# Retention and MLP kernel: one cast moved to VectorE, batch 1's steps and two turns shifted in the weave

## The chip, the cores and the metric

The kernel runs on one core of a Trainium2 chip. Its time is the device time of one execution in microseconds. TensorE (PE in the profile) does the matrix products and the transposes, VectorE (DVE), ScalarE (ACT) and GpSimd (POOL) do elementwise work, and SP issues most of the DMAs; ScalarE issues some too. Each engine works through its own list of instructions in order and waits in front of an instruction until the semaphores that it needs have been raised. So an instruction that waits also holds up everything behind it on its engine.

## The reference

Two layers follow each other. The first is a retention (a linear attention with a decaying state) over 4 batches, 8 heads, 768 positions and 64 channels per head. The second is a mixer: a low-rank mixing over the positions, then an MLP.

```python
for t in range(S):
    state = gamma * state + einsum('bhd,bhe->bhde', k[:, :, t], v[:, :, t])
    y[:, :, t] = scale * einsum('bhd,bhde->bhe', q[:, :, t], state)

# x: y with the heads side by side, [batch, 768, 512]; rank 32, d_model 512
h  = (x.T @ U @ V).T            # mixing over the 768 positions
u  = x + h
out = u + relu(u @ w_ch1) @ w_ch2      # 512 -> 2048 -> 512
```

## The kernel before, in words

The 768 positions of a batch are taken in chunks of 128. Within a chunk, scores of q and k are masked (the masked scores are called `a`) and multiplied by v, and a running state, which is copied from PSUM to SBUF after each chunk, carries what came before. The decay is folded into q and k by the tables `gq` and `gk`.

**The order is written by hand.** The schedule is manual: the order in which the Python code calls the engines is the order in each engine's list.

*Start, batch 0.* Nothing else can run yet, so batch 0 is taken in three blocks of 256 positions (`sc` = 0, 1, 2; lines 784 to 816). Per block, `prep_pair` and `prep_block` (line 240) scale k and q and cast v from fp32 to bf16 in two halves of four heads; the letters passed say which engine takes which half (P GpSimd, D VectorE, A ScalarE). `turn_block` transposes k and q on TensorE. `state_half` (line 346) adds half a block to the state in one PSUM bank and copies it to SBUF on ScalarE; the next `state_half` adds to the same bank and needs that copy to be done, and it needs both halves of the cast v. `score_block` makes the scores and masks them; `mix_block` (line 392) makes the outputs x. Then come the low-rank step and the first up products.

*The weave, batches 0 to 3.* For b = 1 to 4 the loop at line 850 calls `weave` (line 743). It takes the MLP of batch b-1 as a list of pieces with a cost in microseconds (an up product of 128 of the 2048 channels over 512 positions costs 0.864, over the last 256 positions 0.432, a part of a down product 0.864 or 0.874) and puts the steps of other tracks between them: a step with mark d runs before the first piece at which the summed cost has reached d times the total. The total is 41.47 for batch 0's MLP (16 x 0.864 + 16 x 0.432 + 24 x 0.864) and about 39.1 for the others. The tracks are:
- `first`: the low-rank step for u's last two chunks of batch b-1 (`lr_expand`, positions 512 to 767; VectorE adds it to x, line 517), and their turn into `uT`, which the up products over the last 256 positions read. For b = 1 and 2 TensorE turns (`lr_turn_pe`, line 529, with a copy on ScalarE), for b = 3 and 4 a transposing DMA on SP does (`lr_turn`, line 544).
- batch b's own retention, chunk by chunk: `prep_chunk` (line 258, GpSimd), the turn of q and k (`turn_pe` at line 424 for b = 1; a transposing DMA, `turn_dma` at line 432, on ScalarE's queue for b = 2 and on SP's for b = 3), `state`, `score`, `mix`, at the marks `at[i]` plus 0, `lag[0]`, `lag[1]`, `lag[2]`. Below, (b,i) is chunk i of batch b.
- for b = 1, `order_v` (a reordering copy on GpSimd) and eight subtractions on VectorE (`w2_sums`, line 552) that prepare the weights of a seven-product scheme for the later down products.
- the low-rank step of batch b (`lr_open`, `lr_proj`, `lr_expand`, `lr_turn_pair` for b = 1), at marks that follow from the last `at`.

The stores of finished output rows wait in a list. `weave` issues those that were in the list when a piece began right after that piece, so their place between the other DMAs of SP's queue depends on the marks as well: batch 0's rows go out in two stores of 128 KB per chunk on SP.

*Loads.* All inputs pass through a ring of 16 SBUF tiles. `feed_one` (line 123) puts the next load into SP's list each time a tile has been used up, in a fixed order: the blocks of batch 0, U and V, w1, the first chunk of batch 1, w2, then q, k, v of every further chunk.

*Banks.* PSUM has eight banks. The up products of batches 1 to 3 (`up`, line 671) turn over four of them (`RINGS["mlp"]`); three of four results are taken out by a relu on ScalarE (line 684), every fourth by VectorE (line 682). Where such a relu comes late, TensorE finds no free bank.

Of the kernel before, what the change touches and what calls it, by code (L numbers as in the profile page):

```python
# [18 lines left out]
def kernel(  # L19
# [11 lines left out]
    nc = tc.nc  # L31
    P = 128
    B, H, S, D = q.shape
# [18 lines left out]
    SEVEN = 1  # L52
# [70 lines left out]
    def feed_one():  # L123
        if n_fed[0] == len(feed):
            return
        key, src = feed[n_fed[0]]
        n_fed[0] += 1
        if key[0] == "uv":
            nc.sync.dma_start(
                out=Uf.rearrange("p s two r -> p s (two r)"),  # L130
                in_=moe_U.rearrange("(s p two) r -> p s (two r)", p=P, two=2))
            nc.sync.dma_start(
                out=Vf, in_=moe_V.rearrange("r (f t) -> (r f) t", f=NSC))
            return
        t = rin.tile([P, 512], fp32, tag="in", name=f"in_{n_fed[0]}")
        ready[key] = t
        if key[0] in "qkv":
            t = t.rearrange("p (h d) -> p h d", h=H if len(key) == 3 else 4)
        nc.sync.dma_start(out=t, in_=src)

    def take(*key):
        assert feed[n_used[0]][0] == key, (feed[n_used[0]][0], key)
        n_used[0] += 1
        return ready.pop(key, None)
# [24 lines left out]
    def keep_busy(n, fresh=False):  # L169
        if fresh:  # L170
            idle_bank[0] = bank("mlp")
        for i in range(4 * n):
            nc.tensor.matmul(idle_bank[0][:, ts(i % 4, P)], ones[:, :P],  # L173
                             ones[:, :P], start=True, stop=True,
                             skip_group_check=True)
# [53 lines left out]
    for i in range(NST):  # L229
        t = consts.tile([P, 4, P], bf16, name=f"state{i}")  # L230
# [9 lines left out]
    def prep_block(eng, nm, sc, hh):  # L240
        if hh == 0:
            pre[nm, sc] = blk.tile([P, 2, H, D], bf16, tag=nm + "0",
                                name=f"{nm}0_{sc}")
        t = pre[nm, sc][:, :, ds(4 * hh, 4)]
        src = take(nm, 0, sc, hh).rearrange("p (h two d) -> p two h d", h=4,
                                            two=2)
        if nm == "v":
            if eng == "A":
                nc.scalar.activation(t, src, AF.Copy)
            else:  # L250
                nc.gpsimd.tensor_copy(out=t, in_=src)
        else:
            g = (gq0 if nm == "q" else gk0)[:, sc, :, ds(4 * hh, 4), None]
            (nc.gpsimd if eng == "P" else nc.vector).tensor_tensor(
                t, src, g.to_broadcast([P, 2, 4, D]), op=ALU.mult)
        feed_one()
# [16 lines left out]
    def prep_uv():  # L273
        take("uv")
        nc.gpsimd.tensor_copy(out=Uh, in_=Uf)
        nc.gpsimd.tensor_copy(
            out=Vh.rearrange("p (x two t) -> p x two t", x=2, two=2),
            in_=Vf.rearrange("p (x t two) -> p x two t", x=2, two=2))
        feed_one()
# [48 lines left out]
    def turn_block(nm, sc, eng):  # L328
        src = pre[nm, sc]
        t = blk.tile([P, 4, 2, P], bf16, tag=nm + "T0",  # L330
                      name=f"{nm}T0_{sc}")
        np_ = 4 // len(eng)
        for g in range(len(eng)):
            tp = bank("mlp", bf16)
            for p in range(np_):
                for par in range(2):
                    nc.tensor.transpose(
                        tp[:, ds(2 * P * p, 2 * P)].rearrange(
                            "p (x two m) -> p two x m", x=2, two=2)[:, par],
                        src[:, par, ds(2 * (np_ * g + p), 2)], ident)  # L340
            evac(eng[g], t[:, ds(np_ * g, np_)],
                 tp[:, :2 * P * np_].rearrange("p (n x m) -> p n x m", n=np_,
                                               x=2))
        live[nm, sc] = t
# [206 lines left out]
    def part(f, *args):  # L551
        return lambda: f(*args)
# [221 lines left out]
    def prep_pair(nm, sc, engs):  # L774
        for hh in range(2):
            prep_block(engs[hh], nm, sc, hh)
# [7 lines left out]
    for sc in range(NSC):  # L784
        last = sc + 1 == NSC
        keep_busy(3 if sc else 9, fresh=not last)
        turn_block("k", sc, "D")
        keep_busy(0 if sc else 7)
        turn_block("q", sc, "AD" if last else "A")
        prep_pair("v", sc, "PA")  # L790
        if sc:
            state_half(sc - 1, 1)
        else:
            keep_busy(4)
        score_block(sc, 0)
        if last:
            prep_uv()
        else:
            prep_pair("k", sc + 1, "PD")
            prep_block("P", "q", sc + 1, 0)  # L800
            keep_busy(0 if sc else 3)
        if sc:
            score_block(sc, 1, "mlp", "DA")
        else:
            score_block(sc, 1)
        if last:
            state_half(sc, 0)
            mix_block(sc - 1, "AD")
            continue
        prep_block("D", "q", sc + 1, 1)  # L810
        if sc:
            mix_block(sc - 1, "AA")
        keep_busy(4 if sc else 1, fresh=sc > 0)
        state_half(sc, 0)
        if sc == 0:
            nc.vector.tensor_scalar(mask, jmat, srange, None, op0=ALU.is_ge)
# [23 lines left out]
    for c in range(NCB):  # L840
        evac("AD"[c % 2], uTs[0][:, :NLO, c], four(xT[c]))
    keep_busy(3)
    first = [part(lr_expand, 0, 4, 2), part(lr_turn_pe, 0, 4),
             part(lr_expand, 0, 0, 4)]
# [5 lines left out]
    for b in range(1, B + 1):  # L850
        tracks = []
        if b > 1:
            old = b - 1 < SEVEN
            first = [part(lr_expand, b - 1, 4, 2, "qk" if old else "st"),
                     part(lr_turn_pe, b - 1, 4, "qk" if old else "o")
                     if b < 3 else part(lr_turn, b - 1, 4)]
            if not old:
                RINGS["mlp"] = [6, 0, 1, 2]
        tracks.append((first, 0.02, 0.2 if b - 1 < SEVEN else 0.06))
        if b < B:  # L860
            if b == 1:
                at = [0.455, 0.555, 0.61, 0.67, 0.725, 0.78]
                lag = [0.01, 0.035, 0.065]
                turn = turn_pe
                for i in range(AHEAD, NCK):
                    tracks.append(([part(prep_chunk, b, i)], at[i] - 0.1, 1))
                tracks.append(([order_v], at[-1] - 0.05, 1))
                for f, d in zip(w2_sums(0) + w2_sums(2),
                                (0.495, 0.51, 0.53, 0.58, 0.635, 0.65, 0.695,
                                 0.71)):  # L870
                    tracks.append(([f], d, d))
            else:
                for i in range(NCK):
                    prep_chunk(b, i)
                at = [0.04 + 0.085 * i for i in range(NCK)]
                lag = [0.12, 0.17, 0.23] if b == 2 else [0.1, 0.12, 0.2]
                if b == 2:
                    for i, f in enumerate(w2_sums(4) + w2_sums(6)):
                        d = 0.04 + 0.025 * i
                        tracks.append(([f], d, d))  # L880
                turn = turn_dma
            for i in range(NCK):
                for f, d in ((turn, 0), (state, lag[0]), (score, lag[1]),
                             (mix, lag[2])):
                    tracks.append(([part(f, b, i)], at[i] + d, at[i] + d))
            t = at[-1] + lag[2]
            if b == 1:
                tracks += [([part(lr_open, b), part(lr_proj, b)], t + 0.02,
                            t + 0.02),
                           ([part(lr_expand, b, 0, 4)], t + 0.04, t + 0.04),  # L890
                           ([part(lr_turn_pair, b, 0, "A"),
                             part(lr_turn_pair, b, 2, "D")], t + 0.08, t + 0.12)]
            else:
                for fs, d in (([part(lr_open, b), part(lr_proj, b)], 0.03),
                              ([part(lr_grow, b, 0, 4, "st")], 0.06),
                              ([part(lr_add, b, 0, 4, (0, 1))], 0.06),
                              ([part(lr_add, b, 0, 4, (2, 3))], 0.11),
                              ([part(lr_turn, b, 0)], 0.17),
                              ([part(lr_turn, b, 2)], 0.171)):
                    tracks.append((fs, t + d, t + d))  # L900
        weave(mlp_pieces(b - 1), *tracks)
# [29 lines left out]
```

## Time and profile before

| what | us |
|---|---|
| median of 5 runs | 226.78 (225.72 to 226.98) |
| the profiled execution | 226.79 |
| its span, first to last instruction | 225.0 |
| TensorE busy | 213.7 |
| VectorE busy | 147.0 |
| ScalarE busy | 89.1 |
| GpSimd busy | 84.4 |

The page gives the busy time of each engine, a strip of 40 slices of the span, the DMA queues, the chain of work that ended last and the costliest groups of instructions. The trace behind it can be asked for the waits (who waited for whom), for the instructions of a stretch in order of time, and for one line. In those rows "L677" is a line of the kernel, `gT<-mlp` says what is written and read, and `[0.50 <-ACT state L85]` says how long the engine stood before and what is taken to have released it. Releasers are inferred. Further lines that come up: 357 and 444 are the state's matmuls in batch 0 and later, 460 the scores, 465 their masks, 480 the products of masked scores with v in `mix`, 538 the turn of u's first four chunks, 727 VectorE's sum for a finished chunk of batch 0's output, 781 the making of a selection table on VectorE. Helpers share lines: line 85 is every copy out of PSUM on ScalarE, line 87 every one on VectorE.

Time is measured from the span's start: the first up product of the MLP starts at 28.26 us, the first down piece of batch 0 at 51.47, the up products of batch 1 at 82.89, those of batch 2 at 134.8 and those of batch 3 near 181.7.

### The profile page before, as it was taken

To read this page: it belongs to the slowest core of one execution; us is meant where nothing else is said; L and a number is where in the kernel's file an instruction comes from. 1 tells how busy PE (TensorE), PEld (TensorE's weight loads), DVE (VectorE), ACT (ScalarE), POOL (GpSimd) and SP (SyncE) were. 2 spreads that over 40 slices of the span, in tenths; PEclk is the share of its full clock that TensorE was granted. 3 is DMA by queue.
4 is the path that set the end of the run, shared out by engine and by line. 5 is a ranking of instruction groups with operands and counts; after the bars stand their busy time and mean duration, and the time that the engine had idled before them with its cause. 6 is when DMAs were issued, how large, how long until landed. Compare 5 with 4: busy or idle time off the path is not lost. (4 is left out here: it accounts for less than half of the span.)

```text
span 225.0 us, 5592 instructions
## 1 busy us (share of the span) xinstructions
PE 213.7 (95%) x2275; PEld 150.1 (67%) x2275; DVE 147.0 (65%) x292; ACT 89.1 (40%) x183; POOL 84.4 (38%) x123
## 2 busy tenths in 40 slices
PE   6899999999999999699999999999999999999993
PEld 6777844595565454366678884766888855668882
DVE  7678556326873569599997744697777542867452
ACT  3257554464555125376721004776410035551000
POOL 6447878788687856324648202000000000000000
PEclk9999999999999999999999999999999999999999
DMA  6998999999999999999999389921001822000023
GB/s 181 299 291 240 293 368 221 373 338 197 222 208 191 219 207 232 258 192 191 236 208 217 137 177 222 193 44 35 3 0 53 213 112 47 0 1 3 37 106 139
DMA packets 93370, 38.84 MB, mean 173 GB/s; under 512 B 76864, under 2 KB 86176, under 8 KB 93344
## 3 DMA queue, kind: packets, MB, share of 16 engines
q1 hardware_dynamic: 86144, 35.33, 65.4%
q10 hardware_dynamic: 7200, 3.15, 6.7%
q8 instruction: 18, 0.29, 0.6%
q14 instruction: 8, 0.07, 0.1%
HBM read 27.46 MB, written 6.29 MB: 150 GB/s over the span
## 5 line engine op out<-in xcount | busy, mean ns | idle before, releaser
L677 PE MATMUL mlp<-uT,w1b 128*128 128x512 f16 (+1 forms) x512 | 89.7, 326 | 2.4 <-ACT gT L684 2.2
L684 ACT ACTIVATE gT<-mlp 128x512 f16<-128x512 f32 (+1 forms) x94 | 45.6, 490 | 65.9 <-PE mlp L677 60.8
L677 PEld LDWEIGHTS <-w1b 128*128 128x128 f16 x512 | 47.9, 98 | 32.9 <-issue 2.4
L682 DVE TENSOR_SCALAR gT<-mlp 128x512 f16<-128x512 f32 (+1 forms) x34 | 18.9, 555 | 28.0 <-PE mlp L677 28.0
L599 PEld LDWEIGHTS <-gT 128*128 128x128 f16 x288 | 27.6, 98 | 3.6
L268 POOL TENSOR_TENSOR qkd<-in,gk 128x512 bf16<-128x512 f32 x18 | 19.8, 1099 | 22.6 <-DMA in<-in_k_dram 22.4
L465 DVE TENSOR_TENSOR a<-s,mask 128x512 bf16<-128x512 f32 x36 | 23.1, 683 | 6.6 <-PE s L460 6.6
L722 PE MATMUL mlp<-w2b,gT 128*128 128x512 f16 x96 | 23.9, 380 | 0.0
L268 POOL TENSOR_TENSOR qkd<-in,gq 128x512 bf16<-128x512 f32 x18 | 19.4, 1079 | 11.3 <-DMA in<-in_q_dram 8.5
L599 PEld LDWEIGHTS <-gS 128*128 128x128 f16 x216 | 21.0, 98 | 3.2 <-issue 0.5
L85 ACT ACTIVATE x<-o 128x512 f16<-128x512 f32 x20 | 11.9, 595 | 20.6 <-PE o L480 20.2
L599 PE MATMUL A<-w2t,gT 128*128 128x256 f16 x144 | 18.4, 273 | 0.0
L85 ACT ACTIVATE state<-st 64x256 bf16<-64x256 f32 x40 | 15.0, 374 | 4.4 <-PE st L357 3.1
L722 PEld LDWEIGHTS <-gT 128*128 128x128 f16 x96 | 8.1, 98 | 7.7
L266 POOL CAST vd<-in 128x512 bf16<-128x512 f32 x18 | 11.2, 624 | 4.5 <-DMA in<-in_v_dram 3.1
L173 PE MATMUL mlp<-ones 128*128 128x128 bf16 x136 | 10.3, 238 | 1.4 <-DVE ones L166 1.4
L173 PEld LDWEIGHTS <-ones 128*128 128x128 bf16 x152 | 9.9, 107 | 2.2 <-DVE ones L166 1.4
L320 POOL CAST w2b<-in 128x512 f16<-128x512 f32 x16 | 9.8, 614 | 2.9 <-DMA in<-in_moe_w_ch_dram 2.2
L517 DVE TENSOR_TENSOR x<-s,x 128x256 f16<-128x256 f32 (+1 forms) x16 | 8.2, 552 | 4.2 <-PE st L511 1.9
L314 POOL CAST w1b<-in 128x512 f16<-128x512 f32 x16 | 9.6, 613 | 2.8 <-DMA in<-in_moe_w_ch_dram 2.3
L85 ACT ACTIVATE qkT<-qk 128x1024 bf16<-128x1024 bf16 x6 | 6.1, 1023 | 8.2 <-PE qk L424 8.1
L599 PE MATMUL B<-w2b,gT 128*128 128x256 f16 x72 | 9.3, 273 | 0.0
(135 smaller groups left out, 274.8 us busy)
## 6 DMA issues: line engine op xcount, KB each, us to landing
in<-in_moe_w_ch_dram SPq DMA_DIRECT2D x32, 256.0 KB, 6.2
in<-in_k_dram SPq DMA_DIRECT2D x24, 256.0 KB, 5.5
in<-in_q_dram SPq DMA_DIRECT2D x24, 256.0 KB, 5.5
in<-in_v_dram SPq DMA_DIRECT2D x24, 256.0 KB, 5.4
out_dram<-o SPq DMA_DIRECT2D x12, 256.0 KB, 2.0
out_dram<-o SPq DMA_DIRECT2D x12, 128.0 KB, 3.5
out_dram<-o ACTq DMA_DIRECT2D x6, 256.0 KB, 2.6
Uf<-in_moe_U_dram SPq DMA_DIRECT2D x1, 96.0 KB, 4.6
```

The source lines that it names most:

```text
L85: nc.scalar.activation(dst, src, AF.Copy)
L173: nc.tensor.matmul(idle_bank[0][:, ts(i % 4, P)], ones[:, :P], ones[:, :P], start=True, stop=True, skip_group_check=True)
L266: nc.gpsimd.tensor_copy(out=t, in_=src)
L268: nc.gpsimd.tensor_tensor(t, src, g[:, ci, :, None].to_broadcast([P, H, D]), op=ALU.mult)
L314: nc.gpsimd.tensor_copy(out=w1b[:, c, ts(mb, 512)], in_=take("w1", mb, c))
L320: nc.gpsimd.tensor_copy(out=w2b[:, m], in_=take("w2", m))
L465: nc.vector.tensor_tensor(a, four(sp[i]), causal(mask), op=ALU.mult)
L599: nc.tensor.matmul(acc[key, i], lhs[:, m, ts(i, P)], rhs[:, m], start=(fresh and m == 0), stop=(m == NH - 1), skip_group_check=True)
L677: nc.tensor.matmul(g_p[:, :sz], w1b[:, c, ts(m, P)], uTs[b][:, ds(j, nj), c], start=(c == 0), stop=(c == NCB - 1))
L682: nc.vector.tensor_relu(gT[:, m, ds(lo, sz)], g_p[:, :sz])
L684: nc.scalar.activation(gT[:, m, ds(lo, sz)], g_p[:, :sz], AF.Relu)
L722: nc.tensor.matmul(ch, gT[:, m, ts(j, P)], w2b[:, m], start=(m == 0), stop=(m == NM - 1))
```

## The change

Four edits, none of which alters what is computed:
- In the last block of batch 0 (`sc` = 2) the second half of the v cast moves from ScalarE to VectorE. ScalarE's list then has the copy of the state right after its share of the q turn; VectorE's list has the cast after its own share of the q turn and ahead of the masks.
- For b = 1 the marks of the six chunks move from 0.455, 0.555, ... to 0.475, 0.575, ..., that is by 0.02 of the weave. The preparation of chunks 1 to 5, `order_v` and the low-rank step of batch 1 are tied to these marks and move with them.
- For b = 1 the eight subtractions of `w2_sums` move by 0.02 as well.
- The track `first` ends at 0.14 for b = 2 and at 0.1 for b = 3 instead of 0.06. Its second step, the turn of u's last two chunks, comes halfway through the track, so its mark moves from 0.04 to 0.08 (b = 2, from two pieces in to four) and from 0.04 to 0.06 (b = 3, from two pieces in to three). For b = 1 and b = 4 nothing changes there.

```diff
             if eng == "A":
                 nc.scalar.activation(t, src, AF.Copy)
             else:
-                nc.gpsimd.tensor_copy(out=t, in_=src)
+                (nc.vector if eng == "D" else nc.gpsimd).tensor_copy(out=t,
+                                                                     in_=src)
...
         turn_block("q", sc, "AD" if last else "A")
-        prep_pair("v", sc, "PA")
+        prep_pair("v", sc, "PD" if last else "PA")
         if sc:
             state_half(sc - 1, 1)
...
-        tracks.append((first, 0.02, 0.2 if b - 1 < SEVEN else 0.06))
+        tracks.append((first, 0.02, (0.2, 0.14, 0.1, 0.06)[b - 1]))
         if b < B:
             if b == 1:
-                at = [0.455, 0.555, 0.61, 0.67, 0.725, 0.78]
+                at = [0.475, 0.575, 0.63, 0.69, 0.745, 0.8]
                 lag = [0.01, 0.035, 0.065]
...
                 for f, d in zip(w2_sums(0) + w2_sums(2),
-                                (0.495, 0.51, 0.53, 0.58, 0.635, 0.65, 0.695,
-                                 0.71)):
+                                (0.515, 0.53, 0.55, 0.6, 0.655, 0.67, 0.715,
+                                 0.73)):
                     tracks.append(([f], d, d))
```

## The prediction

> **What bounds the kernel now.** First the engines of the page, then the table of waits, then the timeline at the waits that are not matmuls.
>
> ```profile
> PE 213.7 (95%) x2275; PEld 150.1 (67%) x2275; DVE 147.0 (65%) x292; ACT 89.1 (40%) x183; POOL 84.4 (38%) x123
> ```
>
> TensorE works for 213.7 of 225.0 us at full clock. The change takes no matmul away, so only the 11.3 us in which TensorE stands can shrink. Of the rows of the waits with PE in front, these lie near the edits (waiter and releaser, total us, times, longest):
>
> ```profile
> PE mlp L677 <- ACT gT L684: 2.2, 1, 2.2
> PE o L480 <- DVE a L465: 1.2, 4, 0.3
> PE st L357 <- ACT state L85: 0.5, 1, 0.5
> PE o L529 <- DVE x L517: 0.3, 1, 0.3
> ```
>
> The 0.5 is the place of the v cast. Timeline of ScalarE there (start, duration, operation):
>
> ```profile
> 19.95 0.60 ACT L85 ACTIVATE qT<-mlp 128x512 bf16<-128x512 bf16 x1 [0.74 <-PE mlp L337]
> 20.44 0.62 ACT L249 ACTIVATE v<-in 128x512 bf16<-128x512 f32 x1
> 20.96 0.75 ACT L85 ACTIVATE state<-st 64x256 bf16<-64x256 f32 x2
> ```
>
> The state copy waits for the cast ahead of it in the queue. The next state matmuls (L357) reuse its bank and start at 21.77, after 0.50 us of standing.
>
> The 2.2 is in batch 1's up products. Timeline of 91 to 96 us:
>
> ```profile
> 92.03 1.28 POOL L268 TENSOR_TENSOR qkd<-in,gq 128x512 bf16<-128x512 f32 x1 [1.40 <-DMA in<-in_q_dram]
> 92.67 1.30 ACTq L432 DMA_TRANSPOSE qkT<-qkd  x1
> ...
> 94.02 0.60 ACT L684 ACTIVATE gT<-mlp 128x512 f16<-128x512 f32 x1 [3.76 <-POOL qkd L268]
> 94.51 0.77 ACT L85 ACTIVATE state<-st 64x256 bf16<-64x256 f32 x2
> 94.66 1.03 PE L677 MATMUL mlp<-uT,w1b 128*128 128x256 f16 x8 [2.22 <-ACT gT L684]
> ```
>
> ScalarE has nothing to do after 90.26, yet issues chunk (2,1)'s transposing DMA only at 92.67, with the relu that frees TensorE's bank behind it. The printed releaser, GpSimd's qkd, is doubtful: (2,1)'s qkd was written by 76.7. In the built instruction list the DMA also waits for one of eight completion semaphores, which DMAs of both queues take in turn: its previous user is the first half of the store of batch 0's chunk 2. That store was issued at 87.24, and the view of its line for that moment gives:
>
> ```profile
> DMA to landing us min/median/max: 5.3/5.3/5.3
> ```
>
> 87.24 + 5.3 = 92.54; the DMA follows 0.13 later. The first transposing DMA fits as well: store issued 83.26, landed after 3.3 (86.56), issue 86.70. So **TensorE's restart is dated by a landing**: landing + 0.13 + 1.30 (issue) + 0.69 (relu, restart) = landing + 2.12.
>
> **The v cast.** Off ScalarE: 0.62. The state copy can start once its matmuls end (20.01 + 0.62 = 20.63; such a copy followed by 0.03 to 0.04 at 12.57 and 18.44), so 20.66 to 21.42 instead of 21.72: gain 0.30. On VectorE: one 128x512 cast, fp32 to bf16, SBUF to SBUF, not in the trace. Nearest row, L781: SBUF fp32 of 128 elements in 216 ns; if that is two elements a cycle of 0.96 GHz (the Trainium skill's clock and rate for fp32 SBUF copies, "VectorE: DVE Perf Modes"), 384 more elements add 200: 0.42. At one a cycle it would take like the PSUM casts, 0.69. It starts when VectorE's qT ends (20.68), ending 21.10 to 21.37. **Here a rule speaks against the edit**: the Trainium skill, "SBUF — State Buffer", section "SBUF: two separate sides", says that a VectorE operation in a two-port mode and a GpSimd operation take one shared port pair exclusively, the later blocking for the whole instruction. GpSimd casts v's other half at 20.34 to 20.94. The rows of w2t agree: 416 ns at best, but 1.08 at 53.40, ended 0.28 after GpSimd's multiply (53.07 to 54.20). By the row alone v is ready at 21.10, by the rule at 20.94 + 0.28 = 21.22, or at 21.7 if GpSimd's next two casts (to 21.59) get in first. I take 21.22, still ahead of the state copy: L357 starts 0.30 earlier, at 21.47 (ends: 0.0 and 0.5). Behind the cast wait the two masks (21.08 to about 21.22); their reader, the mix at 24.7, has over a microsecond of slack. The input buffer freed later feeds the 15th w1 load, not issued before 27. The first up product comes 0.30 earlier, and w1's casts (first four done by 26.75) still precede it.
>
> **Batch 1's steps**, 0.02 of the weave's 41.47 us, that is one 0.864 us piece later:
> - Nothing is added or removed. Four prep_chunks and order_v move on GpSimd only relative to SP's stores; their order on GpSimd stays, and no step waited for GpSimd before.
> - VectorE's add of output chunk 3 ran just ahead of the masks of (1,5) (72.89, 0.69; masks 73.50), and the mix waited 0.31 at 74.83. A piece later the add is over: gain 0.31. In exchange chunk 1's add and one w2t subtraction come ahead of the masks of (1,2): 0.69 + 0.42 to 1.2 + 1.29 = 2.4 to 3.2, against 2.7 to 2.8 until the mix: loss 0 to 0.4, I take 0.05. The waits of (1,0) (0.29) stay.
> - The projection and turn of batch 1's u get one piece instead of two before batch 2's products: second turn ends about 82.2, VectorE's 0.69 copy 82.9, its first reader 83.3 (clock of before). Cover 0.4; without it, up to 0.3.
> - SP issues the two stores of chunk 0 (1.86 us at 77.60) three loads earlier, so the loads of k, v (2,2) and q (2,3) come up to 1.86 later; from k (2,3) on the queue is the same. SP issues one transfer after the other from 50.8 to 93.4 and the DMA share is mostly about 1.0, so I let all later loads keep their time.
>
> **u's last two chunks.** In the batch-1 products the TensorE turn moves from two to four pieces in: the 0.27 for VectorE's x at 85.38 goes. The copy of uT is then done near 88, its readers begin at 91.4: covered by 3 us. In batch 2's products, a DMA turn, the shift is one piece: SP now issues chunk (3,0)'s transposing DMA first. It has no late operand and goes at about 133.7 instead of 138.91, so u's DMA still leaves at 137.62 (VectorE's x ends 137.56), lands after at most 3.4 (141.0) for readers at 142.67. Zero; if it had to queue behind an issue (1.3 us), still zero.
>
> **What the restart makes of it.** Until the stall TensorE gains 0.30 + 0.31 - 0.05 + 0.27 = 0.83, but it then waits for ScalarE, so these count only if the landing allows it. In the changed list the semaphores rotate: (2,0)'s DMA waits for the load of v (2,3) (80.19 + 4.7 to 5.2) and can go at about 85.2, before the copy of uT; (2,1)'s waits for the **load of q (2,5)**, one transfer ahead of the store. That load was issued at 86.22 and landed after 5.7, at 91.92. New restart 91.92 + 2.12 = 94.04 instead of 94.66: gain **0.62**. Behind it every wait I found is relative to TensorE. Sum: 226.79 (the profiled execution; 225.0 span, 1.79 around it) - 0.62 = 226.17; I say **226.1**. The median shown is 226.78, so the sum holds against it too.
>
> **Rivals.**
> - *The load lands early.* Median landing of the loads between 60 and 95 us: 4.8. Then 91.0, restart 93.1, gain 1.5: **225.2**. For it: stores pulled into SP's gaps (70 to 75 us: DMA share 0.87, SP waiting 2.4 for GpSimd). With no stall at all: 0.83 + 2.22, 223.7. Against: from 75 on the DMAs are full.
> - *The load lands late: slower.* The transposing DMA of (2,0) starts 1.5 earlier, in front of q (2,5) rather than beside it: 256 KB at the 213 GB/s of 86 to 88 us is 1.23. With the longest landing of that stretch, 6.5: 86.22 + 6.5 + 1.23 = 93.95, restart 96.07: **228.2**. Slower from a landing of 92.54 on, by over 0.5% from 93.67. Against: in before that DMA had landed by 92.2 too, so the bytes ahead of q (2,5) are nearly the same.
> - *The change doesn't do what it says here*: the restart is GpSimd's after all, as printed; it stays at 94.66 and all earlier gains vanish in the wait: **226.8**.
>
> **How the numbers follow.** Forecast 0.5 (own range 225.6 to 226.8: landing 91.4 to 92.5), early load 0.25, late load 0.15, GpSimd 0.10. Runs differ by 0.5% (225.72 to 226.98), so less than 1.13 us counts as no change. Faster by over 0.5% (below 225.65): 0.25 and 0.08 of the forecast's edge, 0.33. Slower (above 227.9): 0.15 and 0.02 for what I overlooked, 0.17. The rest 0.50. Range 224.7 to 227.6: it leaves out the stall's full vanishing and the worst of the late load.
>
> **What would show it.** Right: the state copies at 20.7, a VectorE cast of about 0.5 beside them, L357's 0.5 us wait at about 0.2, no wait in front of L529, the wait at 74.83 gone, and (2,1)'s transposing DMA on ScalarE at q (2,5)'s landing, with TensorE restarting 2.0 later and standing 2.4. Wrong: L357 starting after 21.77; a new wait of a mix at (1,2) over 0.4; that DMA issued elsewhere than at q (2,5)'s landing; a wait for DMA in front of the up products near 142.

## The result, and the profile after

| | before | after |
|---|---|---|
| median of the runs compared, us | 226.78 (223.78 to 231.44, 79 runs) | 225.48 (223.63 to 229.06, 42 runs) |
| after / before, 95% interval | | 0.996 (0.9941 to 0.9979) |

By the ratio the change makes the kernel 0.2 to 0.6% faster, about 0.9 us, which is less than the 0.5% taken as the limit of "no change". The forecast was 226.1 us, the range 224.7 to 227.6; the median, 225.48, lies in the range. The ratio, here and below, is taken over the executions within 1.5% of the fastest of their kernel, so it is not the quotient of the medians, which count all of them; and since the execution profiled with this comparison had a lower TensorE clock (0.992), the profile after is that of a later execution of the same kernel: time 224.81, span 222.5 us. In kernels with the v edit all later line numbers are one higher than before (L677 becomes L678, L684 L685, L432 L433).

The engines of the page, and from the table of waits the rows near the edits (waiter and releaser, total us, times, longest):

```profile
PE 213.4 (96%) x2275; PEld 150.4 (68%) x2275; DVE 144.8 (65%) x293; ACT 88.6 (40%) x182; POOL 84.5 (38%) x123
```

```profile
PE mlp L678 <- ACT gT L685: 1.5, 1, 1.5
...
PE o L481 <- DVE a L466: 0.3, 1, 0.3
PE st L358 <- ACT state L85: 0.3, 1, 0.3
PE s L499 <- issue: 0.2, 1, 0.2
```

TensorE works as long as before (213.4 against 213.7). Its large wait in batch 1's up products is 1.5 instead of 2.2, the waits of a mix for its mask are one instead of four, the state's wait is 0.3 instead of 0.5, and the wait of L529 (now L530) for x has gone. One row is new: at L499 TensorE stands 0.2 us, and the trace names nothing that it waited for.

The large wait, as before, in the timeline of ScalarE:

```profile
89.04 0.60 ACT L685 ACTIVATE gT<-mlp 128x512 f16<-128x512 f32 x1 [0.21 <-PE mlp L678]
91.37 1.25 ACTq L433 DMA_TRANSPOSE qkT<-qkd  x1
92.67 0.60 ACT L685 ACTIVATE gT<-mlp 128x512 f16<-128x512 f32 x1 [3.03 <-PE mlp L678]
```

and of TensorE:

```profile
90.79 1.04 PE L678 MATMUL mlp<-uT,w1b 128*128 128x256 f16 x8
93.31 1.03 PE L678 MATMUL mlp<-uT,w1b 128*128 128x256 f16 x8 [1.49 <-ACT gT L685]
```

ScalarE again has nothing to do until it issues (2,1)'s transposing DMA at 91.37, and TensorE restarts 1.94 later. In this kernel the DMA takes over the semaphore of the load of q (2,5). That load was issued at 85.40, and the view of its line for that moment has

```profile
DMA to landing us min/median/max: 5.9/5.9/5.9
```

so it landed at 91.30, and the DMA followed 0.07 later. Landing to restart is 2.01. So far this is the mechanism that the prediction described. What it did not describe is seen only by looking at more executions.

### The profile page after: what moved, and what is told of

It reads as the page before. It is cut to its first block, busy times and chain, and to the rows that moved or that the text cites. A ratio compares the mean times of both kernels' runs of the same rounds, so it can differ in the third digit from the quotient of the medians.

```text
span 226.9 us, 5593 instructions
## 1 busy us (share of the span) xinstructions
PE 214.8 (95%) x2275; PEld 150.9 (67%) x2275; DVE 144.1 (64%) x293; ACT 88.4 (39%) x182; POOL 84.9 (37%) x123
## 5 line engine op out<-in xcount | busy, mean ns | idle before, releaser
L678 PE MATMUL mlp<-uT,w1b 128*128 128x512 f16 (+1 forms) x512 | 91.0, 330 | 3.9 <-ACT gT L685 3.7
L685 ACT ACTIVATE gT<-mlp 128x512 f16<-128x512 f32 (+1 forms) x94 | 45.7, 491 | 68.2 <-PE mlp L678 59.6
L678 PEld LDWEIGHTS <-w1b 128*128 128x128 f16 x512 | 48.6, 99 | 35.0 <-issue 4.1
L267 POOL CAST vd<-in 128x512 bf16<-128x512 f32 x18 | 12.2, 676 | 7.0 <-DMA in<-in_v_dram 4.5
L600 PE MATMUL C<-w2t,gS 128*128 128x256 f16 x72 | 9.3, 273 | 0.0
```

The source lines that it names most:

```text
L600: nc.tensor.matmul(acc[key, i], lhs[:, m, ts(i, P)], rhs[:, m], start=(fresh and m == 0), stop=(m == NH - 1), skip_group_check=True)
L678: nc.tensor.matmul(g_p[:, :sz], w1b[:, c, ts(m, P)], uTs[b][:, ds(j, nj), c], start=(c == 0), stop=(c == NCB - 1))
L685: nc.scalar.activation(gT[:, m, ds(lo, sz)], g_p[:, :sz], AF.Relu)
```

## The experiments

Each kernel below was timed in five rounds beside the kernel before on the same chip, and profiled in one execution. The theory under test is that of **landings**: (2,1)'s DMA waits for the transfer that had its semaphore last, and TensorE for the DMA. The rivals put the wait down to GpSimd, to the order of the DMAs on ScalarE's queue, or to the queue as such.

**1. The change once more, and its parts.** Marks only, v cast only and u turn only are the three parts of the diff, each by itself; v and marks is the change without the hunk of the track `first`. First the change again:

> The changed kernel again, for a trace. Landing theory (TensorE's restart in batch 1's up products is dated by the landing of the transfer whose semaphore ScalarE's transposing DMA of chunk (2,1) takes over): that DMA issues within 0.2 us of the landing of the load of q (2,5), TensorE restarts 2.0 later and stands 2.2 to 2.6; time 0.6 to 0.9 us below before. Carrying theory (the small gains before simply add up): stall still 2.2 or less, 0.8 below before. GpSimd theory: restart follows the end of a GpSimd multiply, time as before.

Measured: median 225.59 (223.77 to 229.13) against 226.29, ratio 0.9975 (0.9937 to 1.0014). The profiled execution took 223.81 with a span of 222.0, and in it the large wait did not exist at all:

```profile
90.25 0.60 ACT L685 ACTIVATE gT<-mlp 128x512 f16<-128x512 f32 x1 [0.21 <-PE mlp L678]
90.33 1.33 ACTq L433 DMA_TRANSPOSE qkT<-qkd  x1
91.71 0.60 ACT L685 ACTIVATE gT<-mlp 128x512 f16<-128x512 f32 x1 [0.86 <-PE mlp L678]
```

Here q (2,5) was issued at 83.89 and landed after 5.3, at 89.19. The DMA did not wait for it; it left right behind the relu ahead of it in the list. The stand of 2.2 to 2.6 that was expected did not come. This execution is the "no stall" end of the prediction (223.7), which its range had left out.

The v cast alone:

```diff
-        prep_pair("v", sc, "PA")
+        prep_pair("v", sc, "PD" if last else "PA")
```

(with the choice of `nc.vector` for "D" in `prep_block`)

> Only the v cast on VectorE. The semaphore of (2,1)'s transposing DMA is that of before (first half of the store of batch 0's chunk 2). Landing theory: L357's wait falls from 0.5 to 0.2, the first up product is 0.3 earlier, the stall in batch 1's up products grows from 2.2 to 2.5, time as before (ratio 1.000). Carrying theory: stall 2.2, time 0.3 us below (0.9987).

Measured: 226.22 against 226.29, ratio 0.9994 (0.9951 to 1.0038). The state's wait fell to 0.21, yet the first up product was not earlier; TensorE stood for 0.85 at L499, of which more below. The large wait was 1.35, not the 2.5 expected.

The marks alone:

```diff
-                at = [0.455, 0.555, 0.61, 0.67, 0.725, 0.78]
+                at = [0.475, 0.575, 0.63, 0.69, 0.745, 0.8]
```

(and the eight marks of `w2_sums`, 0.02 later each)

> Only the marks of batch 1 and of the subtractions, 0.02 later. Semaphore as before. Landing theory: the 0.31 wait of the mix of (1,5) goes, up to 0.4 may come at (1,2), the stall grows by what was won; time as before (0.998 to 1.001; less only if the two stores pulled ahead make the later store land earlier). Carrying theory: 0.26 below (0.9988).

Measured: 226.85 against 226.29, ratio 1.0023 (0.9972 to 1.0074). The wait of the mix of (1,5) is gone from its trace.

The u turn alone:

```diff
-        tracks.append((first, 0.02, 0.2 if b - 1 < SEVEN else 0.06))
+        tracks.append((first, 0.02, (0.2, 0.14, 0.1, 0.06)[b - 1]))
```

> Only the later turn of u's last two chunks. It alone rotates the semaphores: (2,1)'s transposing DMA follows the load of q (2,5), one transfer earlier. Landing theory: the 0.27 wait ahead of L529 goes, restart 0.6 us earlier than before, stall 1.9 to 2.0; time 0.6 below (0.997): of the three parts the only one with a gain. Carrying theory: 0.27 below (0.9988), stall 2.2.

Measured: 226.32 against 226.29, ratio 0.9967 (0.992 to 1.0013). Its twelve times fall into two groups: three between 223.3 and 223.7, nine between 226.1 and 227.1, none between them. The profiled execution, 223.32, is of the first group and has no large wait.

The v cast and the marks together:

> The v cast and the marks, without the u edit: (2,1)'s DMA waits for the store as before. Landing theory: TensorE arrives 0.5 earlier and stands 0.5 longer; ratio 0.999 to 1.001. Carrying theory: 0.9976.

Measured: 225.87 against 226.72, ratio 0.9963 (0.9921 to 1.0005); no large wait in the profiled execution (224.52), where 2.7 was expected. Here the DMA still follows the store, as before, and that store landed after 4.0 instead of 5.3.

All five intervals hold 1. The ratios alone can't rank the parts: the scatter between executions of one kernel, 4 to 5 us from the lowest to the highest, is larger than any part. The traces can, since each part has its own place in them. This table cuts each profiled span at the first up product of batch 0, at the first one of batch 1, at the first one over its last 256 positions, and at the first one of batch 2:

| kernel | to first up | to batch 1 | to the 256 | to batch 2 | to the end | wait of L677 or L678 |
|---|---|---|---|---|---|---|
| before | 28.26 | 54.63 | 8.52 | 43.38 | 90.2 | 2.22 |
| v only | 30.09 | 54.63 | 8.52 | 42.22 | 90.2 | 1.35 |
| u only | 28.95 | 54.63 | 7.91 | 39.82 | 90.2 | none |
| v and marks | 29.28 | 54.75 | 8.52 | 39.89 | 90.3 | none |
| change, again | 29.74 | 54.35 | 7.91 | 39.84 | 90.2 | none |
| change, as shown above | 28.54 | 54.35 | 7.90 | 41.61 | 90.1 | 1.49 |

The marks take 0.28 out of the second column, in "marks only" as well (54.35). The u turn takes 0.61 out of the third. The last column repeats to within 0.2. The first scatters from execution to execution, the fourth holds the large wait, and the 54.75 of v and marks is taken up below.

**2. Which transfer dates the DMA?** Three kernels move one DMA or the other to another semaphore. In the first, (2,0)'s DMA is called ahead of u's turn as in the change, but (2,1)'s keeps the semaphore of the store:

```diff
-        tracks.append((first, 0.02, 0.2 if b - 1 < SEVEN else 0.06))
+        tracks.append((first, 0.02, (0.2, 0.061, 0.06, 0.06)[b - 1]))
```

> Before, with the turn of u's last two chunks in its old place, two pieces in, but called after the transposing DMA of (2,0) instead of ahead of it. That DMA takes the semaphore of the load of v (2,3) as in the change and goes about 1 us earlier; that of (2,1) keeps the one of before (store of batch 0's chunk 2, first half). Landing theory: restart at that store's landing + 2.1, no gain (ratio 0.999 to 1.001), stall as often as before. Rival (the early first DMA, or simply the order of the two on ScalarE, brings the gain): 0.997, like the u edit alone.

Measured: 226.22 against 226.72, ratio 1.0013 (0.9978 to 1.0048); wait 0.9, DMA at 91.87, 0.05 behind the landing of the store. The early first DMA does not bring the second one forward.

In the other two, (2,1)'s turn comes later, and its DMA behind a later store; first in the change, then in the kernel before:

```diff
-                for f, d in ((turn, 0), (state, lag[0]), (score, lag[1]),
+                for f, d in ((turn, 0.06 if b == 2 and i == 1 else 0), (state, lag[0]), (score, lag[1]),
```

> The change, with the transposing DMA of (2,1) 0.06 of the weave later: two relus, a state copy and one short relu come ahead of it on ScalarE. It then follows the second half of the store of chunk 2, so its own landing is later, not earlier. Landing theory with ScalarE's queue as the carrier: the relus that free TensorE's banks no longer stand behind it, the stall is gone or under 1 us even in executions with a late landing; median 224.2 to 224.8, spread narrower, ratio to before 0.989 to 0.994. GpSimd or carrying theory: as the change, 0.996.

Measured: 224.37 (223.18 to 226.0) against 226.72, ratio 0.9943 (0.9899 to 0.9987); waits 2.0 and 0.4 in the profiled execution, where under 1 was expected.

> Before, with only that later DMA. Landing theory: the 2.2 us stall shrinks to under 1, what stays is 0.8 us of small waits that the change removes; ratio to before 0.991 to 0.995, so better than the whole change. GpSimd theory: 1.000.

Measured: 226.03 against 226.72, ratio 0.998 (0.994 to 1.0021); waits 0.4 and 0.3; the ratio expected, 0.991 to 0.995, did not come. In both the DMA again came 0.1 to 0.2 behind the landing of the transfer whose semaphore it took over. This table is the main finding; times are of the profiled executions:

| kernel | transfer ahead on the semaphore | issued | landed | (2,1)'s DMA | TensorE stood |
|---|---|---|---|---|---|
| before | store, chunk 2, first half | 87.24 | 92.54 | 92.67 | 2.2 |
| v only | same | 87.92 | 93.52 | 93.64 | 1.4 |
| marks only (clock 0.994) | same | 87.69 | 92.69 | 92.75 | 2.0 |
| v and marks | same | 87.03 | 91.03 | 91.15 | 0 |
| tie | same | 86.62 | 91.82 | 91.87 | 0.9 |
| u only | load of q (2,5) | 85.22 | 89.52 | 89.82 | 0 |
| change, again | same | 83.89 | 89.19 | 90.33 | 0 |
| change, as shown above | same | 85.40 | 91.30 | 91.37 | 1.5 |
| change, in the comparison (clock 0.992) | same | 88.20 | 94.10 | 94.23 | 3.7 |
| later turn, in the change | store, chunk 2, second half | 89.9 | 93.5 | 93.69 | 2.0 |
| later turn, in before | store, chunk 3, first half | 89.0 | 93.3 | 93.48 | 0.4 |

In the first seven of the rows in which the DMA waited, it goes 0.05 to 0.13 behind the landing, whichever transfer it is; the last two landings are known to 0.1 only. The view gives the time to landing to 0.1; by the semaphore updates of the traces themselves the distance is 0.10 in all nine. In u only and the change again the transfer had landed earlier, and ScalarE came to the DMA later. GpSimd and the order of the DMAs fall. But the landing itself is no constant of a kernel. Without the two rows at a lower clock, the load of q (2,5) lands between 89.2 and 91.3, since it is issued over a stretch of 1.5 us and takes 4.3 to 5.9; the store of chunk 2's first half lands between 91.0 and 93.5. The large wait is a draw: from nothing to 2.2 us with the store, from nothing to 1.5 with the load.

**3. A place that has no draw.** If that is so, the DMA should be put where its semaphore's last transfer has long landed: just behind (2,0)'s, on the semaphore of a store of chunk 1 that is issued three transfers before q (2,5).

```diff
-                for f, d in ((turn, 0), (state, lag[0]), (score, lag[1]),
+                for f, d in ((turn, -0.05 if b == 2 and i == 1 else 0), (state, lag[0]), (score, lag[1]),
```

> The change, with the turn of (2,1) pulled forward to just behind that of (2,0) (mark 0.075 instead of 0.125). Its transposing DMA then takes over the semaphore of the second half of the store of batch 0's chunk 1, issued some 3 us ahead of the load of q(2,5). Landing theory: that store has landed by 87 to 89 even in an execution with late landings, so both DMAs go one behind the other on ScalarE by 89.5, and the stall behind a late landing (0 to 3.7 us in the runs so far) is gone from the profiled execution; at most 1 us of standing near 88 where the two issues (2.6 us) come together. Median 224.2, 0.989 of before, and a narrower spread of the executions than the change's 223.8 to 229.1. Rival (the stall is the channel's: whatever transfer ScalarE issues there waits until the queue drains): the stall stays, DMA after 91, median as the change, 225.5.

Measured: 224.58 (222.97 to 227.88) against 226.24, ratio 0.9969 (0.9933 to 1.0005). The profiled execution has no large wait, (2,1)'s DMA at 87.03, and the shortest span of all, 221.2. With it the rival that a DMA issued there waits until the queue drains falls as well. The narrower spread that was expected did not come: 4.9 us. Beside it ran the later turn and the change, each once more:

> The kernel of e6 once more (the change, with the turn of (2,1) 0.06 of the weave later, behind the first half of the store of chunk 2's second half). Its 0.9943 of before had an interval of 0.9899 to 0.9987, and its profiled execution stood for 2.4 us. If landings decide, a later place of the same kind wins nothing in the mean: 225.3, 0.995 as the change itself. If the later place is really better than the change's: 224.4, below the change on the same chip by 1 us.

Measured: 224.88 (223.52 to 227.51), ratio 0.9979 (0.9938 to 1.002). By the ratio the gain of 0.9943 did not repeat; by the median it did in part, for 224.88 is 0.9 below the change beside it, which follows. In the profiled execution the DMA went at 92.38, when the store of chunk 2's second half had landed 0.6 before, and TensorE stood for 0.3.

> The change again, on the same chip as the two others: 225.5, 0.996 of before; profiled stall anywhere between 0 and 3.7 us, restart 2.0 to 2.1 us after the transposing DMA of (2,1), and that DMA 0.1 to 0.2 after the landing of q(2,5) where it stood waiting for it.

Measured: 225.79 (223.48 to 229.53), ratio 0.9979 (0.9934 to 1.0024); the profile is the one shown as after. The early turn was then run a second time:

> The kernel of e9 once more. If the early turn takes the wait for a landing away for good, its executions again lie close together, with a median of 224.5 (0.992 of before) and no stall in the profiled one. If e9's median was luck, 225.5 like the change.

Measured: 223.66 (222.34 to 226.4) against 226.29, ratio 0.9917 (0.9872 to 0.9962). The profiled execution, 225.16, did have waits, 0.39 and 0.80. The timeline, SP's store rows and others left out:

```profile
87.41 3.04 ACTq L433 DMA_TRANSPOSE qkT<-qkd  x1
...
92.06 2.01 PE L678 MATMUL mlp<-uT,w1b 128*128 128x256 f16 x16 [0.39 <-ACT gT L685]
...
95.32 1.47 ACTq L433 DMA_TRANSPOSE qkT<-qkd  x1
...
97.28 1.02 PE L678 MATMUL mlp<-uT,w1b 128*128 128x512 f16 x4 [0.80 <-ACT gT L685]
```

(2,1)'s DMA now goes at 87.41, 0.1 behind its store's landing (84.4 + 2.9) and 0.15 behind the end of (2,0)'s issue, but its own issue held ScalarE for 3.04 instead of 1.3. And the next one, (2,2)'s, has become the late one: it left at 95.32, when the first half of chunk 3's store had landed (89.3 + 6.0). In the first execution of this kernel (2,2)'s DMA followed that landing too, at 93.69 (88.0 + 5.6), and TensorE did not stand for it. The draw has moved on to the next transposing DMA, where it is smaller. So the expectation of no stall in this execution failed, and that of a lower median held: the early turn's two medians, 224.58 and 223.66, lie below all three of the change (225.48, 225.59, 225.79). But so do the later turn's two, 224.37 and 224.88, although its place has the draw. The early turn's ratios to before do not clear those of the change by their intervals. So a lead of about 1 us over the change is likely and not shown, and that it comes from the missing draw is not shown either.

## Why the prediction was right, and where it was not

**The v cast: its size was right.** From the state's matmuls ahead of the copy to those behind it (L357) was 1.76 before (in the five profiles without the edit 1.76 three times, 1.83 and 2.16) and is 1.47 or 1.48 in all nine with it: 0.28 gained of 0.30. The cast, which the trace of before did not have, was sized at 0.42 alone, and 0.28 past GpSimd's end by the rule. In the v-only kernel it came after GpSimd's cast and took 0.43. In the profile after the two began together:

```profile
20.75 0.89 DVE L251 CAST v<-in 128x512 bf16<-128x512 f32 x1
20.75 0.60 POOL L251 CAST v<-in 128x512 bf16<-128x512 f32 x1
20.83 0.77 ACT L85 ACTIVATE state<-st 64x256 bf16<-64x256 f32 x2 [0.42 <-PE st L358]
```

VectorE's ends at 21.64, 0.29 after GpSimd's. In v and marks VectorE's began first:

```profile
20.83 0.43 DVE L251 CAST v<-in 128x512 bf16<-128x512 f32 x1
...
20.87 0.85 POOL L251 CAST v<-in 128x512 bf16<-128x512 f32 x1
```

Now GpSimd's takes 0.85 instead of 0.60 and ends 0.46 after VectorE's; there the trace names GpSimd's half of v as what the state's matmuls waited for (0.29). This is the exclusive port pair of the Trainium skill ("SBUF — State Buffer", section "SBUF: two separate sides"), where the first to start has it for its whole instruction; both orders are in these traces. The cover that the prediction named, ScalarE's copy of the state, ends at 21.60 in the profile after, and L358 starts at 21.65: just long enough for a cast that ends at 21.64.

**What it brings was not there.** "The first up product comes 0.30 earlier" is the step that failed. From those matmuls to the first up product took 6.5 to 7.0 in the five profiles without the edit (6.49, 6.50, 6.50, 6.90, 6.99) and 6.7 to 7.5 in the nine with it, 0.36 more in the mean (0.29 without the two at a lower clock). TensorE stands within the 24 products of L499 (L498). Its timeline, before and after:

```profile
26.27 0.52 PE L498 MATMUL s<-x,Ub 128*32 128x128 f16 x24
```

```profile
26.15 0.41 PE L499 MATMUL s<-x,Ub 128*32 128x128 f16 x16
26.78 0.29 PE L499 MATMUL s<-x,Ub 128*32 128x128 f16 x8 [0.22 <-issue]
```

It has x and Ub, and the trace shows no releaser. From the first of the 24 to the next instruction takes 0.46 where they run without a break (before, the tie, marks only), 0.87 and 0.96 in the other two without the edit, and 0.66 to 1.49 in the nine with it.

The records of the DMA queues point to what it waits for: its own instructions. Queue q8 carries instructions only, by its row of the page before (packets, MB, share of 16 engines):

```profile
q8 instruction: 18, 0.29, 0.6%
```

These 18 transfers of 16 KB are spread over the span as TensorE works through its 4550 matmuls and weight loads, one to about 250 of them. The third one ends between 24.5 and 26.8 us. In all eleven profiles in which TensorE stands at L499, it stands in front of the same product, the 17th, and goes on 1.4 to 1.6 after the end of that transfer; in the three without a stand it reached the 17th product 1.5 to 2.0 after it. So in those eleven the first up product is dated by this transfer, as far as the traces tell; no run moved it. It began 1.4 to 2.9 after the start of L357's matmuls in the five profiles without the edit and 2.5 to 3.3 after it in the nine with the edit, so the 0.28 did not reach the first up product; the v-only ratio of 0.9994 fits. Whether the edit itself makes the transfer later or chance did, no run settles.

**The marks: right.** 0.28 net against 0.26. In three of the nine profiles with the marks (v and marks, and one each of the early and the later turn) the second column is about 54.75 instead of 54.35: the loss at (1,2), for which 0 to 0.4 was given and 0.05 taken, is then at its upper end. Timeline of v and marks:

```profile
63.13 1.28 DVE L553 TENSOR_TENSOR w2t<-w2b 128x512 f16<-128x512 f16 x1
...
64.33 1.28 DVE L466 TENSOR_TENSOR a<-s,mask 128x512 bf16<-128x512 f32 x2
...
65.67 0.29 PE L481 MATMUL o<-vd,a 128*128 128x64 bf16 x4 [0.24 <-DVE a L466]
```

The subtraction ahead of the masks takes 1.28 beside a GpSimd multiply; in the six profiles without the loss it took 0.41 to 0.87.

**The u turn: right in its mechanism, wrong in its size.** 0.27 was taken from the row of the wait; 0.61 came. TensorE's timeline, before:

```profile
84.08 1.04 PE L677 MATMUL mlp<-uT,w1b 128*128 128x512 f16 x4
85.38 0.79 PE L529 MATMUL o<-ident,x 128*128 128x128 f16 x8 [0.27 <-DVE x L517]
86.01 5.34 PE L677 MATMUL mlp<-uT,w1b 128*128 128x512 f16 x24
```

and after:

```profile
84.07 2.76 PE L678 MATMUL mlp<-uT,w1b 128*128 128x512 f16 x12
86.67 0.61 PE L530 MATMUL o<-ident,x 128*128 128x128 f16 x8
87.11 3.62 PE L678 MATMUL mlp<-uT,w1b 128*128 128x512 f16 x16
```

After, twelve products take 2.60 from the first start to the next instruction, so four take 0.87; before, they take 1.30. TensorE stood for 0.43, not 0.27: the row counts from a matmul's modelled end, which lies 0.17 past the moment at which the next could start. Another 0.19 stood inside the eight transposes (0.63 from their start to the next product, 0.44 after), whose last quarter of x came late. The Trainium skill says the same of the ends ("Perfetto Trace Analysis", section "Tensor Engine Instruction (MATMUL, LD_WEIGHTS)"): the profiler estimates them. Starts are measured.

**The restart: the rule held, the date did not.** "Landing + 2.12" measured 2.01 to 2.13. The mis-sized term is "5.7, at 91.92": one landing of before taken over as a fixed date, where two executions of the changed kernel had 89.19 and 91.30. From that followed the wrong conclusion that the stall always takes what is gained ahead of it. "Runs differ by 0.5%" was too small as well: it came from five runs, and the 79 of the comparison lie between 223.78 and 231.44. By place the change gains 0.28 + 0.61 = 0.9 in the marks and the turn, and the cast's 0.28 did not show at the first up product; the measured ratio makes 0.9 (0.5 to 1.3). That the two agree is no proof, since in an execution with a stall part of the 0.9 is lost in it. The forecast of 0.62 lay near by luck: its reason does not hold.

**"Behind it every wait I found is relative to TensorE"** was not so. Without the large wait the fourth column is 39.8; the kernel before has 43.38, 1.3 more than its wait of 2.22 explains. Two waits of batch 2's mixes are part of it, in before

```profile
112.37 0.29 PE L480 MATMUL o<-vd,a 128*128 128x64 bf16 x4 [0.29 <-DVE a L465]
117.27 0.29 PE L480 MATMUL o<-vd,a 128*128 128x64 bf16 x4 [0.31 <-DVE a L465]
```

Such rows are also in v only, marks only, the tie and the later turn in before, and in none of the profiles without the stall. With 0.17 more for each of the three stands, as above, they make up 1.1 of the 1.3. So a stall of TensorE can cost more than its own length. It need not: the change's profile with the wait of 1.49 has no such rows, and its fourth column exceeds 39.84 by 0.3 more than the wait.

**The other rivals.** The early landing is what the change's two profiles at full clock show, once with a rest of the wait and once without any; as a date of the kernel it falls like the forecast's, since it is a draw. GpSimd as releaser falls with the table of landings. b = 3's turn cost nothing, as predicted, but for 0.2 in the early turn's first profile in front of the products near 139.

## What to carry to other kernels

Before a trace's time of landing goes into a sum, look at it in several executions: a wait for a transfer on a full DMA system is a distribution, and one profile shows one draw of it. When a DMA on one queue leaves late with its data ready, look for the transfer of another queue whose completion semaphore it takes over; where it is placed in the list decides that. Size a TensorE stand from start to start, against the same instructions where they run without a break, and not from the row of the wait. Where it stands and no releaser is named, compare the date with the transfers of the instruction queue.

## What the runs showed of the hardware

The same 256 KB load, in the same place of the list, was issued between 83.89 and 85.40 and landed after 4.3 to 5.9 us, at full clock. The issue of a transposing DMA held ScalarE's queue for 1.25 to 1.56 us, but for 1.79 to 3.04 in the five cases in which it went within 0.2 us of the end of another one's issue, and for 2.45 and 2.25 in one case each of marks only and the tie, which did not. The eight completion semaphores are taken in turn by the DMAs of SP and ScalarE (19 or 20 times each in the profile before), and (2,1)'s DMA, where it waited for its semaphore, left 0.10 after the landing of the transfer ahead on it. TensorE's instructions come in transfers of 16 KB, and the stand behind the third of them took up to 1.0 us. The first up product came anywhere from 28.3 to 30.1 us, nearly as large a scatter as that of the large wait at full clock, 0 to 2.2.
